# Block-sparse attention with a gated projection behind it: a reserve in the planner's times for work that waits, and another rank for one sequence's value means

## The chip, the cores and the metric

The kernel runs on one core of a Trainium2 chip. The metric is the device time of one execution in microseconds; the number given for a kernel is the median of its runs. A program fixes the order of the instructions on every engine before anything runs. On the chip each engine works through its own list in order and waits where an operand isn't there yet. PE is TensorE, DVE VectorE, ACT ScalarE, POOL GpSimd, and SP is SyncE, whose queue issues the transfers.

## The reference

```python
q, k, v: [4, 8, 768, 64]          # sequences, heads, positions, head width
k_sum = k.reshape(B, H, 24, 32, D).max(axis=3)
v_sum = v.reshape(B, H, 24, 32, D).mean(axis=3)
scores_l = where(|i - j| < 16, scale * q @ k.T, -1e9)
scores_s = scale * q @ k_sum.T + log(32)
a = softmax(concat([scores_l, scores_s], -1))
x = a @ concat([v, v_sum], 2)     # then [B*S, H*D] = [3072, 512]
out = ((x @ w_a) * (x @ w_b)) @ w_out   # w_a, w_b [512, 1536], w_out [1536, 512]
```

Each position sees the positions nearer than 16 and 24 summaries, one for each block of 32 positions: the largest key and the mean value. All is float32. The kernel gets that precision from TensorE with a high and a low part of each factor and three matmuls for each product.

## The kernel before

**Units and tiles.** The 3072 tokens are cut into nine units. The first sequence has three units of two tiles of 128 tokens; the other three sequences have two units of three tiles each. For each unit there is an attention part (scores, softmax, transposes, products with the values) and a projection part of twelve items, one for each 128 columns of `d_ff`. An item has two up projections (line 1046), the elementwise product and its split (`h L1081` and `gl L1086` on VectorE, `g L1078` and `gh` on ScalarE for units of two tiles) and the down projection into the output banks (line 1123). The attention part of a tile is computed beside the items of an earlier unit. Its scores are `c L637`, its products `o L790`.

**The summaries of the values.** `prep_values(b)` computes the value means of sequence b, for four heads at a time. Loads bring values (`S<-in_v`), GpSimd adds them (line 561) and scales the sum (line 588). Four small transfers for the four heads (`S<-vm`) then put the means into the room `summed(b)`, so there are eight for a sequence. `bring` loads the values of a tile into the window `vw` (`vw<-in_v`), and for the first tile of a sequence two transfers (`vw<-S`) put the means into the rows of the window behind the values. The products of that tile read them.

**Queries and transposes.** For each tile, `blocks` loads the queries in 16 small pieces (`qin<-in_q`) and VectorE transposes them (`qT`, line 998). The scores of the tile read `qT`. VectorE scales and masks the scores into `s` (line 666), which frees their banks.

**What sets the order.** The class `Work` gathers operations with an engine, a rank, an estimated duration (`takes`), a delay until others can use the result (`then`) and, for transfers, a rate. `emit` plans the program with these estimates. An operation gets a time `est` at which its operands are there by the plan. For the engine that is free first, `emit` takes the operation of best rank (lowest number) among those whose `est` is not over 0.15 us away:

```python
            op = min(
                (o for o in choices(engine) if o.est <= now + 0.15),
                key=lambda o: (o.rank, o.est, o.index),
            )
```

A table `ORDER` names the first operations of each engine by number; behind these the planner decides. Rank 0 (`CHAIN`) is the chain of copies and multiplications inside an item. On SyncE value loads have rank 97, queries 98 and the `S<-vm` transfers rank 99, the two `vw<-S` rank 97.

Of the kernel before, what the change touches and what calls it, by code (L numbers as in the profile page):

```python
# [16 lines left out]
AX = mybir.AxisListType  # L17
LOG32 = 3.4657359027997265
NEG = -1.0e9

# [39 lines left out]
class Work:  # L62
# [27 lines left out]
    def emit(self):  # L90
        fixed = {e: list(reversed(x)) for e, x in ORDER.items()}
        listed = {i for x in ORDER.values() for i in x}
        ready = {}
        wire = 0.0

        def choices(e):
            ops = ready.get(e, [])
            if fixed.get(e):
                return [o for o in ops if o.index == fixed[e][-1]]
            return [o for o in ops if o.index not in listed]  # L100

        for op in self.ops:
            if not op.left:
                ready.setdefault(op.engine, []).append(op)
        left = len(self.ops)
        while left:
            now, engine = min(
                (max(self.free.get(e, 0.0), min(o.est for o in choices(e))), e)
                for e in ready if choices(e)
# [5 lines that stand above are left out]
            ready[engine].remove(op)  # L115
            left -= 1
            if fixed.get(engine):
                fixed[engine].pop()
            start = max(now, op.est)
            end = self.free[engine] = start + op.takes  # L120
            if op.rate:
                wire = max(wire, end + 1.0) + op.then / op.rate
                end = wire + 0.9
            else:
                end += op.then
            op.start = start
            op.fn()
            for o in op.next:
                o.left -= 1
                same = 0.0 if op.engine == "PE" else 0.12  # L130
                o.est = max(o.est, start + op.takes + same if o.engine == op.engine else end)
                if not o.left:
                    ready.setdefault(o.engine, []).append(o)

# [2 lines left out]
def attention_moe(  # L137
# [19 lines left out]
    NS = S // BLK  # L157
# [21 lines left out]
    def sb(shape, name, dtype=F32):  # L179
        return const.tile(shape, dtype, tag=name, name=name)  # L180
# [28 lines left out]
    def mask_kind(i):  # L209
        for e in range(2):  # L210
            es = slice(e * QT, (e + 1) * QT)

            for c0, n, w in ((0, WIN, 0),) if e == 0 else ((0, 32, 0), (32 + NS, 64, 32)):
# [6 lines left out]
                for step, base, per_query in bounds:  # L220
                    nc.gpsimd.affine_select(
                        out=sl, in_=sl, compare_op=ALU.is_ge, fill=NEG, base=base,
                        pattern=[[step, n]], channel_multiplier=per_query,
# [11 lines left out]
    vbuf = [sb([P, H, D], f"vw{e}") for e in range(2)]  # L235
# [26 lines left out]
    late = []  # L262
# [18 lines left out]
    def summed(b):  # L281
        return spaces["S1"][4 * NS : 5 * NS, 3 * CV :].rearrange("p (h d) -> p h d", d=D)
# [32 lines left out]
    def pool(rank, takes, reads, writes, fn):  # L315
        work.add("POOL", rank, takes, 0.13, reads, writes, fn)

    def load(rank, kb, rate, reads, writes, out, in_):
        work.add(
            "SP", rank, 0.45, kb, reads, writes,  # L320
            lambda: nc.sync.dma_start(out=out, in_=in_), rate=rate,  # L321
        )
# [227 lines left out]
    def prep_values(b):  # L550


        T = 8

        at, keys, rank = (0, ["S1.0", "S1.1"], LATER) if b == 1 else (3, ["S1.3"], 50)
        x = spaces["S1"][: 4 * NS, at * CV :]

        def add(n, out, i0, i1, writes):
            pool(
                rank, 0.15 + n / 450, (), writes,  # L560
                lambda: nc.gpsimd.tensor_tensor(out=out, in0=i0, in1=i1, op=ALU.add),  # L561
            )

        room = ["S1.3"] if b == 1 else []
        work.add("-", 0, 0, 0, (), room, lambda: None)
        for hg in range(2):
            vv = v[b, 4 * hg : 4 * hg + 4].rearrange("h (n t) d -> (h n) t d", t=BLK)
            y, pk = vm[: 4 * NS, hg], f"vm{hg}"
            for i in range(BLK // T):
                j = i % len(keys)  # L570
                load(
                    90, 197.0, 150, (), [keys[j]],
                    x[:, j * T * D : (j + 1) * T * D].rearrange("p (t d) -> p t d", d=D),
                    vv[:, i * T : (i + 1) * T, :],
                )
                if j == len(keys) - 1:
                    n = len(keys) * T * D // 2
                    while n > D:
                        add(n, x[:, :n], x[:, :n], x[:, n : 2 * n], keys)
                        n //= 2  # L580
                    if i == j:
                        add(n, y, x[:, :n], x[:, n : 2 * n], keys + [pk])
                    else:
                        add(n, x[:, :n], x[:, :n], x[:, n : 2 * n], keys)
                        add(n, y, y, x[:, :n], keys + [pk])
            pool(
                rank, 0.37, (), [pk],
                lambda y=y: nc.gpsimd.tensor_scalar(
                    out=y, in0=y, scalar1=1.0 / BLK, scalar2=None, op0=ALU.mult
                ),  # L590
            )
            for h in range(4):
                load(
                    99, 6.0, 20, [pk] + room, [VS[4 * hg + h]],
                    summed(b)[:, 4 * hg + h], y[h * NS : (h + 1) * NS],
                )

# [227 lines left out]
    VK = [f"v{i}" for i in range(5)]  # L825
    VS = [f"vs.{h}" for h in range(H)]
# [136 lines left out]
    def attention(u):  # L963

        b, t0, n = chunks[u]
        rank = rank_of(u)
        banks, vbank = ["c0", "c1"], ["c0", "c1"] if u == FILL else ["o3"] * n
        if t0 == 0:
            prep_keys(b)
            prep_values(b)  # L970
        qk = []
        old = [f"qin.{c}.{r}" for c in range(NP) for r in range(0, P, 32)]
        if n == G:
            for c in range(NP):
                qk += blocks(
                    98, f"qin.{c}", qin[:, c, :], q, b, c, t0 * P, ["lo8"] if u == FILL else ()
                )

        def place(i):
            return slice((t0 + i) % 2 * P, ((t0 + i) % 2 + 1) * P)  # L980

        def bring(i):
            load_values(b, t0 + i, vbuf, VK[:3], 97)
            if t0 == 0 and i == 0:
                for e, r0 in ((0, WIN), (1, 32)):
                    load(97, 49.0, 100, VS + (["S1.3"] if b == 1 else []), [VK[3 + e]], vbuf[e][r0 : r0 + NS], summed(b))

        def begin(i):
            keys = list(qk)
            if n != G:  # L990
                for c in range(NP):
                    keys += blocks(
                        98, f"q{(t0 + i) % 2}.{c}", qin[:, c, place(i)], q, b, c, (t0 + i) * P, (),
                        old if chunks[u - 1][2] == G and i < 2 else (),
                    )
            dve(
                rank_of(u, t0 + i) - 0.05 * (u > FILL), 0.62, keys, ["qT"],
                lambda: nc.vector.transpose(out=qTs, in_=qin[:, :, place(i)]),
            )
            scores(u, t0 + i, qTs, "qT", s0, SK, banks, lead=lead.pop() if lead else None)  # L1000

        def turned(i):
            transposes(u, t0 + i, s0, SK, banks)

        def end(i):
            pt = (pown, [PU, ["S0.2", "S0.3"]]) if u == FILL and i else None
            return u, t0 + i, vbuf, VK, vbank[i], pt

        if u == FILL:

            yield
            bring(0)
            begin(0)
            turned(0)
            yield
            begin(1)
            pool(rank, 0.9, (), ["S0.2", "S0.3"], lambda: nc.gpsimd.memset(pown, 0.0))
            turned(1)
            yield
            values(*end(0))  # L1020
            bring(1)
            values(*end(1))
        else:
            for i in range(n):
                begin(i)
                bring(i)
                turned(i)
                if u == FILL + 1:
                    values(*end(i))
                else:  # L1030
                    lead.append(products(*end(i)))
        if u == NU - 1:
            reads, bk, fn, split = lead.pop()
            pe(-1, 1.1, reads, [bk], fn)
            split()
        yield
# [203 lines left out]
```

## Time and profile before

| what | value |
| --- | --- |
| median of three runs | 673.56 us (675.9, 673.56, 672.68) |
| the profiled execution | 675.08 us, its span 673.3 us, mean granted clock of TensorE 0.983 |
| PE busy | 646.2 us, 96% of the span |
| PE weight loads busy | 603.3 us, 90% (beside the matmuls) |
| DVE busy | 401.9 us, 60% |
| ACT busy | 244.5 us, 36% |
| POOL busy | 156.4 us, 23% |

The span is cut into 40 slices on the page, and each digit tells a slice's busy share, or for the clock its granted share of full speed, in tenths (9 is 90% or more). A timeline row gives the start and the duration in microseconds, then the line, the operation, the tiles written and read, and how many instructions are taken together; in brackets stands how long the engine was idle before them and what ended that. A row of the chain of waits gives one piece of the work that ended last. SPq is the time in which SyncE issues a transfer, not the transfer itself.

### The profile page before, as it was taken

The numbers are of one execution on the slowest core, as the hardware profiler recorded it, in microseconds if no ns is written. First come the engines' busy times: TensorE is split into PE (matmuls) and PEld (weight loads), VectorE is DVE, ScalarE is ACT, GpSimd is POOL, SyncE is SP. The second block draws the span as 40 slices with busy tenths as digits, with TensorE's granted clock in tenths as the row PEclk, the third lists the DMA queues.
The fourth block names the chain that finished last, engine by engine and source line by source line (L and its number), as shares of the span: only waits on it lengthen the run. The fifth ranks groups of instructions, "written<-read, shape, count | busy, mean of one in ns | idle before, by whom it ended". The sixth has DMA issues, their size and how long they took to land.

```text
span 673.3 us, 13320 instructions
## 1 busy us (share of the span) xinstructions
PE 646.2 (96%) x5096; PEld 603.3 (90%) x5096; DVE 401.9 (60%) x880; ACT 244.5 (36%) x725; POOL 156.4 (23%) x236
## 2 busy tenths in 40 slices
PE   6699999999699999999999999999999999999997
PEld 5589898998689999999999999999999999999996
DVE  5787799967177777477776865776762542222212
ACT  4798685333134331233333413333331411121111
POOL 5767466351033444211111100101110100000000
PEclk9689999999989999999999999999999999999999
DMA  9997995532134235332222431222000200010001
GB/s 206 255 301 182 359 259 95 114 93 63 27 85 105 62 67 98 75 91 42 40 40 41 94 61 36 39 63 55 11 21 1 70 1 1 0 48 1 1 0 48
DMA packets 154664, 54.73 MB, mean 81 GB/s; under 512 B 134745, under 2 KB 147289, under 8 KB 154601
## 3 DMA queue, kind: packets, MB, share of 16 engines
q1 hardware_dynamic: 154456, 53.75, 33.4%
q8 instruction: 40, 0.66, 0.4%
q14 instruction: 24, 0.19, 0.1%
q10 hardware_dynamic: 144, 0.13, 0.1%
HBM read 47.12 MB, written 6.29 MB: 79 GB/s over the span
## 4 chain that ended last, share of the span: by engine, by line
PE 77%; SPq 7%; DMA 6%; DVE 5%; issue 2%; ACT 1%; POOL 1%; POOLq 0%; ACTq 0%; DVEq 0%
PE h L1046 46%; PE o L1123 24%; SPq L321 7%; PE o L790 3%; DMA raw<-in_moe_w_a_dram 3%; PE c L637 2%; DMA raw<-in_moe_w_out_dram 2%; DVE S L774 1%; POOL w L403 1%; DVE pt L774 1%; DVE c L387 1%; DVE S L395 1%; DVE h L1081 1%; PE o L624 0%; PE o L637 0%
## 5 line engine op out<-in xcount | busy, mean ns | idle before, releaser
L1046 PE MATMUL h<-x,w 128*128 128x384 f32 (+1 forms) x2292 | 392.0, 307 | 0.0
L1046 PEld LDWEIGHTS h<-x,w 128*128 128x128 f32 x2292 | 342.9, 190 | 4.7 <-issue 0.3
L1123 PE MATMUL o<-w,gh 128*128 128x512 f32 x498 | 123.8, 383 | 0.1
L1109 DVE TENSOR_TENSOR h<-h,g 128x384 f32<-128x384 f32 x71 | 40.2, 566 | 134.8 <-PE h L1046 134.4
L1111 ACT CAST gh<-h 128x384 fp32r<-128x384 f32 x71 | 34.0, 479 | 214.2 <-DVE h L1109 209.1
L774 DVE STREAM_TRANSPOSE pt<-s 32x256 f32<-32x256 f32 x228 | 99.3, 436 | 20.7 <-POOL s L729 10.0
L1123 PEld LDWEIGHTS o<-w,gh 128*128 128x128 f32 x498 | 90.6, 189 | 11.5 <-issue 1.9
L729 POOL TENSOR_TENSOR s<-s,nml 128x480 f32<-128x480 f32 x44 | 43.3, 988 | 236.2 <-DVE nml L725 187.6
L1046 PE MATMUL h<-late,w 128*128 128x384 f32 x288 | 93.9, 326 | 0.0
L703 ACT ACTIVATE s<-s,nml 128x120 f32<-128x120 f32 x160 | 61.3, 386 | 33.7 <-DVE nml L674 33.7
L1123 PE MATMUL o<-w,gl 128*128 128x512 f32 x249 | 68.7, 381 | 0.0
L1046 PEld LDWEIGHTS h<-late,w 128*128 128x128 f32 x288 | 54.4, 189 | 0.9
L1106 ACT COPY g<-h 128x384 f32<-128x384 f32 x72 | 34.5, 480 | 55.1 <-PE h L1046 54.3
L1123 PEld LDWEIGHTS o<-w,gl 128*128 128x128 f32 x249 | 46.6, 189 | 7.4 <-DVE gl L1086 0.6
L1114 DVE TENSOR_TENSOR gl<-h,gh 128x384 fp32r<-128x384 f32 x71 | 39.4, 555 | 22.1 <-ACT gh L1111 21.3
L561 POOL TENSOR_TENSOR S<-S 96x256 f32<-96x256 f32 (+3 forms) x58 | 33.2, 572 | 67.6 <-DMA S<-in_v_dram 64.6
L666 DVE SCALAR_TENSOR_TENSOR s<-c,mask 128x480 f32<-128x480 f32 x40 | 26.1, 652 | 20.5 <-PE c L637 20.3
L403 POOL TENSOR_TENSOR w<-S,w 128x512 fp32r<-128x512 f32 x24 | 30.7, 1285 | 9.9 <-ACT w L400 8.8
L1123 PE MATMUL o<-w,x 128*128 128x512 f32 x117 | 30.9, 400 | 0.6 <-POOL w L403 0.5
L703 ACT ACTIVATION_READ_ACCUMULATOR s<-s,nml 128x1 f32 x160 | 30.3, 189 | 0.0
L1078 ACT COPY g<-h 128x256 f32<-128x256 f32 x36 | 13.4, 373 | 46.1 <-PE h L1046 46.1
L387 DVE TENSOR_SCALAR c<-raw 128x512 int32<-128x512 uint32 x36 | 27.3, 761 | 1.6 <-DMA raw<-in_moe_w_a_dram 1.0
(130 smaller groups left out, 527.0 us busy)
## 6 DMA issues: line engine op xcount, KB each, us to landing
raw<-in_moe_w_b_dram SPq DMA_DIRECT2D x12, 512.0 KB
raw<-in_moe_w_a_dram SPq DMA_DIRECT2D x12, 512.0 KB
raw<-in_moe_w_out_dram SPq DMA_DIRECT2D x12, 512.0 KB
out_dram<-S SPq DMA_DIRECT2D x23, 256.0 KB
qin<-in_q_dram SPq DMA_DIRECT2D x288, 16.0 KB
S<-in_v_dram SPq DMA_DIRECT2D x24, 192.0 KB
kin<-in_k_dram SPq DMA_DIRECT2D x38, 100.0 KB
vw<-in_v_dram SPq DMA_DIRECT2D x17, 192.0 KB
```

Of the source, the lines that this page charges most:

```text
L321: lambda: nc.sync.dma_start(out=out, in_=in_), rate=rate,
L387: dve(rank, 0.66, [raw], [bk], lambda: nc.vector.tensor_scalar(out=z.bitcast(I32), in0=word(0).bitcast(U32), scalar1=2.0**-29, scalar2=7.0 ...
L403: lambda eng=nc.vector if near else nc.gpsimd: eng.tensor_tensor(out=half(1), in0=t, in1=half(0).bitcast(F32), op=ALU.subtract),
L703: lambda h=h, c=c, more=more: nc.scalar.activation(y[h][:, c, :], x[h][:, c, :], AF.Exp, bias=m[:, 0, h, c : c + 1], scale=1.0, **more,),
L729: lambda h=h, r=r: nc.gpsimd.tensor_tensor(out=y[h], in0=y[h], in1=r[:, :, None].broadcast_to([P, NP, COLS]), op=ALU.mult,),
L774: lambda js=js, qs=qs, rs=rs: nc.vector.transpose(out=pv[js, rs, qs], in_=sv[qs, rs, js]),
L1046: nc.tensor.matmul(ps, w[:, c, part, :], inputs_of(u, xpart)[:, :, c].rearrange("p g (a b) -> p g b a", a=2), start=(i == 0), stop=(i == n ...
L1106: act(CHAIN, 0.13 + W / 1030, ["h0"], gk, lambda: nc.scalar.copy(out=g, in_=pa))
L1109: lambda: nc.vector.tensor_tensor(out=pb, in0=pb, in1=g, op=ALU.mult),
L1111: act(CHAIN, 0.16 + W / 1030, [bk], [ghk], lambda: nc.scalar.copy(out=gh, in_=pb))
L1114: lambda: nc.vector.tensor_tensor(out=gl, in0=pb, in1=gh.bitcast(F32), op=ALU.subtract),
L1123: nc.tensor.matmul(bank[ok[j]], (gh if first else gl)[:, j * P : (j + 1) * P], w[:, :, part, :].rearrange("p (z a) n -> p z n a", a=2), st ...
```

## The change

The planner gets a constant `SLACK`. When an operation ends and another one waits for it on another engine, the time at which the second one can start by the plan is set later: by 0.35 us if the first is work of an engine, and by 2.0 us if it is a transfer. This holds only for times beyond 70 us of the plan, and neither for operations of rank 0 nor for those of SyncE. Apart from that, for sequence 1 (the second one) the eight `S<-vm` get rank 89 in place of 99 and the two `vw<-S` rank 89.5 in place of 97, so that both stand before the queries with 98. In the changed kernel all lines behind the planner are four higher.

```diff
--- before.py
+++ after.py
@@ -17,6 +17,7 @@
 AX = mybir.AxisListType
 LOG32 = 3.4657359027997265
 NEG = -1.0e9
+SLACK = (0.35, 2.0)
 
 
 
@@ -128,7 +129,10 @@
             for o in op.next:
                 o.left -= 1
                 same = 0.0 if op.engine == "PE" else 0.12
-                o.est = max(o.est, start + op.takes + same if o.engine == op.engine else end)
+                late = start + op.takes + same if o.engine == op.engine else end
+                if late > 70 and o.rank and o.engine != "SP" and o.engine != op.engine:
+                    late += SLACK[op.rate > 0]
+                o.est = max(o.est, late)
                 if not o.left:
                     ready.setdefault(o.engine, []).append(o)
 
@@ -591,7 +595,7 @@
             )
             for h in range(4):
                 load(
-                    99, 6.0, 20, [pk] + room, [VS[4 * hg + h]],
+                    89 if b == 1 else 99, 6.0, 20, [pk] + room, [VS[4 * hg + h]],
                     summed(b)[:, 4 * hg + h], y[h * NS : (h + 1) * NS],
                 )
 
@@ -983,7 +987,7 @@
             load_values(b, t0 + i, vbuf, VK[:3], 97)
             if t0 == 0 and i == 0:
                 for e, r0 in ((0, WIN), (1, 32)):
-                    load(97, 49.0, 100, VS + (["S1.3"] if b == 1 else []), [VK[3 + e]], vbuf[e][r0 : r0 + NS], summed(b))
+                    load(89.5 if b == 1 else 97, 49.0, 100, VS + (["S1.3"] if b == 1 else []), [VK[3 + e]], vbuf[e][r0 : r0 + NS], summed(b))
 
         def begin(i):
             keys = list(qk)
```

Every engine executes the same instructions as before, in another order. The explicit order comes first in both, and the first differences stand behind it.

SyncE's queue around the second sequence's means, before (`S_146<-vm` are the means, `S_146<-in_v_dram` the values that they are computed from, `qin` the queries, `out_dram` the second unit's output in the row that follows the 30 queries):

```order
L321 DMA S_146<-vm 24x64 x3
L321 DMA S_146<-in_v_dram 96x512 x2
L321 DMA S_146<-vm 24x64
L321 DMA qin<-in_q_dram 32x4x32 x30
L321 DMA out_dram<-S_147 128x512 x2
L321 DMA qin<-in_q_dram 32x4x32 x34
L321 DMA S_146<-vm 24x64 x4
L321 DMA vw_129<-S_146 24x512
L321 DMA vw_130<-S_146 24x512
```

The same place now:

```order
L325 DMA S_146<-vm 24x64 x4
L325 DMA vw_130<-in_v_dram 64x8x64
L325 DMA qin<-in_q_dram 32x4x32 x2
L325 DMA S_146<-in_v_dram 96x512 x2
L325 DMA out_dram<-S_147 128x512 x2
L325 DMA qin<-in_q_dram 32x4x32 x11
L325 DMA S_146<-vm 24x64 x4
L325 DMA vw_129<-S_146 24x512
L325 DMA vw_130<-S_146 24x512
```

Between the second four `S<-vm` and the loads of their values there are 11 queries now, where there were 64. The two queries of the shown row with x2 belong to the second sequence's second tile; they stood ahead of the first four `S<-vm` and now come behind them.

TensorE's queue at the products of the second sequence's first tile (`o_74<-pt,vw_129`, the first two rows of eight), before:

```order
L1123 MATMUL o_71<-w_870,gh 128x512 x2
L1123 MATMUL o_72<-w_870,gh 128x512 x2
L1123 MATMUL o_71<-w_870,gl 128x512
L1123 MATMUL o_72<-w_870,gl 128x512
L1046 MATMUL h_75<-x,w_1064 128x256 x12
L1046 MATMUL h_75<-x,w_1020 128x256 x12
L790 MATMUL o_74<-pt,vw_129 64x64 x2
L790 MATMUL o_74<-pt,vw_130 64x64 x2
```

The same products now:

```order
L1050 MATMUL h_76<-x,w_693 128x256 x12
L1050 MATMUL h_76<-x,w_706 128x256 x12
L1127 MATMUL o_71<-w_699,gh 128x512 x2
L1127 MATMUL o_72<-w_699,gh 128x512 x2
L1127 MATMUL o_71<-w_699,gl 128x512
L1127 MATMUL o_72<-w_699,gl 128x512
L794 MATMUL o_74<-pt,vw_129 64x64 x2
L794 MATMUL o_74<-pt,vw_130 64x64 x2
```

They stood behind the up projection with `w_1064` and now follow the down projection with `w_699`, which is four items' places further up. The scores of the third tile, which stood ahead of that down projection, come behind the products.

TensorE's queue at the scores of the second sequence's second tile (the last two rows of eight, `c_77` and `c_78`) and what follows them, before (`o_73` and `o_74` are the second unit's last down projection):

```order
L637 MATMUL c_77<-kT,qT 64x120 x2
L637 MATMUL c_78<-kT,qT 64x120 x2
L1046 MATMUL h_75<-x,w_450 128x256 x12
L1046 MATMUL h_75<-x,w_399 128x256 x12
L1123 MATMUL o_73<-w_1393,x 128x512 x2
L1123 MATMUL o_74<-w_1393,x 128x512 x2
L1123 MATMUL o_73<-w_1393,x 128x512
L1123 MATMUL o_74<-w_1393,x 128x512
```

The same place now:

```order
L1127 MATMUL o_73<-w_1393,x 128x512 x2
L1127 MATMUL o_74<-w_1393,x 128x512 x2
L1127 MATMUL o_73<-w_1393,x 128x512
L1127 MATMUL o_74<-w_1393,x 128x512
L1050 MATMUL h_75<-x,w_450 128x256 x12
L1050 MATMUL h_75<-x,w_399 128x256 x12
L641 MATMUL c_77<-kT,qT 64x120 x2
L641 MATMUL c_78<-kT,qT 64x120 x2
```

The last down projection of the second unit and the up projection with `w_450` (shown whole) have gone ahead of all eight rows of these scores.

## Rows read from the trace of the kernel before

**Rows 1.** The page: busy time of TensorE, and its granted clock in 40 slices.

```profile
PE 646.2 (96%) x5096; PEld 603.3 (90%) x5096; DVE 401.9 (60%) x880; ACT 244.5 (36%) x725; POOL 156.4 (23%) x236
...
PEclk9689999999989999999999999999999999999999
```

**Rows 2.** Stretches of the span: length, busy of PE, PEld, DVE, ACT, POOL, clock, DMA.

```profile
170.00:187.00 17.00, 11.45 (x103) 10.78 (x103) 2.62 (x7) 2.61 (x7) 0.03 (x1) 0.89 0.18 36
187.00:204.00 17.00, 17.00 (x168) 15.30 (x165) 13.05 (x29) 5.63 (x22) 6.99 (x13) 0.91 0.31 75
400.00:663.00 263.00, 263.00 (x1821) 249.80 (x1820) 108.52 (x232) 66.17 (x193) 12.47 (x14) 1.00 0.10 24
```

**Rows 3.** Waits of TensorE: us in total, times, longest.

```profile
PE o L790 <- DMA vw<-S: 5.6, 2, 5.4
```

**Rows 4.** Timeline of SyncE, 100 to 190 us.

```profile
138.96 2.50 SPq L321 DMA_DIRECT2D S<-vm  x3
141.55 0.92 SPq L321 DMA_DIRECT2D S<-in_v_dram  x2
...
143.38 15.74 SPq L321 DMA_DIRECT2D qin<-in_q_dram  x30
...
160.12 18.36 SPq L321 DMA_DIRECT2D qin<-in_q_dram  x34
178.58 3.05 SPq L321 DMA_DIRECT2D S<-vm  x4
182.90 1.48 SPq L321 DMA_DIRECT2D vw<-S  x2
```

**Rows 5.** The chain that ended last, 66 to 190 us: start, us, what.

```profile
151.17 0.43 SPq L321
151.65 1.72 DMA qin<-in_q_dram
...
183.67 2.07 DMA vw<-S
```

**Rows 6.** Stretches of 2 us, columns as in the other stretches.

```profile
162.00:164.00 2.00, 0.71 (x9) 0.29 (x12) 1.97 (x4) 0.62 (x3) 0.00 (x0) 1.00 0.25 43
...
184.00:186.00 2.00, 0.70 (x8) 0.54 (x10) 0.00 (x0) 0.00 (x0) 0.00 (x0) 0.50 0.36 98
```

**Rows 7.** Timeline of TensorE, 100 to 200 us.

```profile
106.13 1.05 PE L637 MATMUL c<-kT,qT 64*64 64x120 f32 x32 [1.53 <-DVE qT L998]
...
148.85 1.05 PE L637 MATMUL c<-kT,qT 64*64 64x120 f32 x32
...
152.61 1.46 PE L1123 MATMUL o<-w,x 128*128 128x512 f32 x6
...
162.66 0.42 PE L637 MATMUL c<-kT,qT 64*64 64x120 f32 x4 [0.46 <-DVE s L666]
163.91 1.04 PE L637 MATMUL c<-kT,qT 64*64 64x120 f32 x28 [0.83 <-DVE s L666]
...
166.28 5.52 PE L1046 MATMUL h<-x,w 128*128 128x256 f32 x48
...
185.11 0.48 PE L790 MATMUL o<-pt,vw 120*64 120x64 f32 x4 [5.37 <-DMA vw<-S]
185.78 1.76 PE L790 MATMUL o<-pt,vw 120*64 120x64 f32 x28 [0.19 <-DMA vw<-S]
187.47 2.76 PE L1123 MATMUL o<-w,x 128*128 128x512 f32 x6
...
196.82 1.15 PE L790 MATMUL o<-pt,vw 120*64 120x64 f32 x32
```

**Rows 8.** Timeline of GpSimd, 136 to 190 us.

```profile
145.01 3.02 POOL L561 TENSOR_TENSOR S<-S 96x512 f32<-96x512 f32 x4 [5.05 <-DMA S<-in_v_dram]
...
148.51 0.37 POOL L588 TENSOR_SCALAR vm<-vm 96x64 f32<-96x64 f32 x1
```

**Rows 9.** Timeline of VectorE, 148 to 165 us.

```profile
153.45 0.71 DVE L998 STREAM_TRANSPOSE qT<-qin 128x512 f32<-128x512 f32 x1 [2.74 <-DMA qin<-in_q_dram]
```

## The prediction

> **What bounds the kernel now.** I read the busy shares of the page first. TensorE is at work for 646.2 us of a 673.3 us span, and its granted clock is high in all but a few slices [rows 1]. A change that leaves the number of matmuls alone can therefore win only time in which TensorE stands idle or runs at its lower clock. Next I cut the span into stretches of 17 us, to see where that time lies. From 187 us to 663 us TensorE is busy in every microsecond. The stretch of 170 to 187 has 11.45 us of 17 [rows 2]. The ramp before 66 us is held by the explicit order, which the change leaves as it is. The third view is the list of TensorE's waits: the longest behind the ramp is for the transfer `vw<-S`, the second sequence's value means on their way into the value window [rows 3].
>
> The queue of SyncE says why they are late. The first half of the means was issued around 139 us and its sums' second half was loaded at 141.55. Then come 30 query blocks, two outputs and 34 more query blocks, and only at 178.58 the second four `S<-vm` [rows 4]. GpSimd had those means ready at 148.51 + 0.37 = 148.9 us [rows 8]. So they sat for 30 us behind work of better rank. `vw<-S` reads what they write, so it is issued at 182.90, and lands 2.07 us after its second issue [rows 4, 5]. TensorE waits 5.37 + 0.19 us, and runs at half clock afterwards [rows 6, 7].
>
> **What the change does and what each part costs.** Every engine gets the instructions that it had. Only their order differs, and only behind the explicit order.
>
> *The means.* The eight `S<-vm` now rank ahead of queries. By the new order the second four have 182 transfers ahead of them on SyncE, not 219, and none is skipped or doubled. Of those 182, 180 are the ones that stood first before too, and two are the second unit's outputs. The 180 were out at about 157.7: the 34 queries begin at 160.12 after 185 transfers, and the three queries and two outputs before that take some 2.4, at 0.475 us from one query to the next [rows 4, 5]. With the two outputs the means can be issued at 158.7. They need their sums. The two loads that feed these have 17 more transfers ahead than before, in places that came at 151.2, so they end at 152.1 [rows 5]. GpSimd started 2.5 us after such a pair and took 3.87 us [rows 4, 8], which gives 158.5, just in time. The outputs need their copies, and by the new order the second unit's last down projection stands ahead of an up projection of 2.8 us and a score group, so the copies come earlier as well. From the first `S<-vm` to the products took 185.78 - 178.58 = 7.2 us [rows 4, 7], so the window is whole at **165.9**.
>
> TensorE would meet the products there at **167**: in the new order they follow the down projection with `w_699`, ahead of which the up projection with `w_693` now stands. That began at 166.28, right behind the other, and is half of 5.52 [rows 7]; so 166.28 + 2.7, less the third tile's scores that have gone behind the products (1.05) and their waits (1.29), less 1.0 and plus 1.5 for the two scores below. That is a margin of about 1 us. The wait of **5.56 us goes**; the bounds are 0 and 2 us of it left.
>
> *The clock.* The six down matmuls behind the products took 2.76 us where six others took 1.46, and 28 product matmuls 1.76 where 32 take some 1.1, so 28 some 0.95 [rows 7]. That is 1.30 + 0.81 = **2.1 us** at half clock, after a stretch in which TensorE did nothing [rows 6, 7]. Waits of 0.46, 0.83 and 1.53 us left the clock whole (1.00 in 162 to 164, with 1.29 us idle) [rows 6, 7]. So if the new waits are of that size, the 2.1 us go too. The Trainium skill (TensorE: Matmul & The Clock Gate, "A second HAM failure mode: psum-queue depth-cycling") says that frequent short idles between groups of matmuls can throttle the clock as well; by that, the short waits left here could cost what the long one did, and the sum would be 2.1 us smaller. The row of 162 to 164 speaks against it.
>
> *Scores of the third tile.* They waited 0.46 + 0.83 us for VectorE to read the banks [rows 7]. With the reserve the planner sets them behind the products, some 7 us later, while VectorE's order is nearly the same. **1.29 us go**; bounds 0.5 and 1.3.
>
> *First scores of the third unit.* They waited 1.53 us for their transposed queries [rows 7]. By the new order four matmuls of a down projection stand ahead, two thirds of a group of 1.46. **1.0 us go**; bounds 0 and 1.53.
>
> *What comes new.* Three queries of the second tile move from issue 139 to 141 (about 133 us) to 157, 165 and 166, behind the four first means. Issue 166 was out by 151.1, landing took 1.7 us and the transpose takes 0.7 [rows 5, 9]: the scores can start at 153.5. TensorE got to them at 148.85; the down projection (to 154.1) and the up projection now go first, so it comes at 154.1 - 1.05 - 1.0 = 152.0 [rows 7]. **A new wait of 1.5 us**; bounds 0 and 3, since VectorE waited 2.74 us in the same way for the next tile's queries, unseen by TensorE [rows 9].
>
> *The reserve behind 187 us.* It reorders work there too, but TensorE has no idle time to win. A new order costs something only if TensorE meets an operand that isn't there. The reserve plans work for other engines later, never earlier, and the projections' own copies are excluded, so I cost it at nothing. The cover is TensorE's backlog of down and up projections; without it each late operand costs its lateness.
>
> **The sum.** 5.56 + 2.1 + 1.29 + 1.0 - 1.5 = 8.45, so 8.5 us. The profiled execution took 675.08 us, so it becomes 666.6. The median of the three runs is 1.52 us below that execution, so I predict **665.1 us**.
>
> **The rivals.**
> *The wait only shrinks.* The margin of 1 us is thin on both sides. SyncE loses about 1 us now and then: its 30 queries took 15.74 us where 30 x 0.475 is 14.25 [rows 4]. The sums come only 0.2 us before their transfer. If the means are late by 4 us, TensorE idles for 3 there, since it now arrives some 17 us sooner. It gains 5.5 us in all: 669.6 at the profiled execution's level less 1.5, so 668. If the wait is again as long as 5.4, the clock falls again too: 665.1 + 5.4 + 2.1 = 672.6, no gain to speak of. I give 0.11 to 667 to 670, and 0.06 to the second.
> *Short waits throttle.* By the rows of 162 to 164 it doesn't happen; if it did, 2.1 us stay: 667.2. Chance 0.04.
> *The change does not reach the bound.* The planner goes by its own times, so on the chip the same means could wait elsewhere; but the order itself shows them 37 places further up. 673.6, chance 0.03.
> *Slower.* SyncE issues in order. The first four `S<-vm` now stand ahead of two of the second tile's queries. If GpSimd's sums are late, SyncE stands at the first `S<-vm`, and all queries with it; VectorE then stands at the transpose of those queries, and the multiplications (`h L1081`) that feed TensorE are queued behind it. It has happened here in small: VectorE idled 2.74 us for queries [rows 9]. The price is 1 us for each microsecond beyond the 1.5 already counted, plus 2.1 for the clock. It makes the kernel slower by over 0.5% from 9.8 us on (8.5 + 3.4 - 2.1), so if the queries land behind 162.6 in place of 152.8; 12 us would give 679. For it: GpSimd waited 5.05 us for a load in this stretch [rows 8]. Against it: the first means could be issued at 138.96 before [rows 4], and now go at about 146. Chance 0.05.
>
> **How the numbers follow.** My forecast has 0.71; its own range, from the bounds of the terms, is 663 to 668. A measurement of this kernel can tell about 0.5%, 3.4 us. Faster means under 670.2: 0.71 + 0.11 + 0.04 - 0.03 for the upper end = 0.83. Same is 0.06 + 0.03 + 0.03 = 0.12, slower 0.05. Leaving out the cases above, the range is **662.8 to 670**.
>
> **What would show it.** In the changed profile the wait of `o L790` for `vw<-S` should be gone or under 2 us, the clock 1.00 from 170 to 204, `S<-vm` issued near 159, a wait of 1 to 2 us at the scores near 152 for `qT`, and no wait for `s L666` at 162. Behind 200 us TensorE stays full. A wait of over 3 us for `vw<-S` near 167 makes the first rival right; idle time behind 200 us makes my cost of the reserve wrong, and idle VectorE with TensorE behind it near 150 the last one.

## The result

The changed kernel takes **663.47 us** (median of four runs, 663.15 to 664.12), the kernel before 673.12 us on the same chip: a ratio of 0.9853, with a 95% interval of 0.982 to 0.9885. Measured again beside the experiments it took 663.08 us (0.9846, 0.9821 to 0.9872). The forecast was 665.1 us, in a range of 662.8 to 670.

| the profiled execution | before | changed |
| --- | --- | --- |
| its time / its span | 675.08 / 673.3 us | 664.12 / 662.3 us |
| PE busy | 646.2 us, 96% | 642.8 us, 97% |
| mean granted clock | 0.983 | 0.992 |

The page of the changed kernel, TensorE's busy time and clock; they answer to [rows 1]:

```profile
PE 642.8 (97%) x5096; PEld 600.8 (91%) x5096; DVE 401.8 (61%) x880; ACT 243.6 (37%) x725; POOL 156.3 (24%) x236
...
PEclk9789999999999999999999999999999999999999
```

TensorE's waits behind the ramp, in the changed kernel (total, times, longest). What was 5.6 us for `vw<-S` in [rows 3] is 0.5:

```profile
PE c L641 <- DVE qT L1002: 0.7, 1, 0.7
PE c L641 <- DVE nml L723: 0.6, 1, 0.6
PE o L794 <- DMA vw<-S: 0.5, 1, 0.5
```

The stretches that answer to [rows 2]. From 170 to 187 us TensorE now works in every microsecond, at full clock:

```profile
153.00:170.00 17.00, 16.45 (x144) 15.00 (x143) 11.96 (x28) 5.72 (x22) 7.33 (x12) 1.00 0.21 40
170.00:187.00 17.00, 17.00 (x198) 15.73 (x197) 13.65 (x33) 6.75 (x27) 5.66 (x11) 1.00 0.35 73
187.00:204.00 17.00, 17.00 (x154) 16.09 (x154) 11.69 (x29) 6.42 (x25) 6.65 (x11) 1.00 0.39 83
400.00:652.00 252.00, 252.00 (x1759) 239.29 (x1758) 107.86 (x231) 64.02 (x189) 12.58 (x15) 1.00 0.11 26
```

SyncE's timeline in the changed kernel, for [rows 4]. Eleven queries stand between the loads of the values at 148.55 and the second four `S<-vm`, which are issued at 156.38 and no longer at 178.58:

```profile
148.55 0.83 SPq L325 DMA_DIRECT2D S<-in_v_dram  x2
...
150.85 5.40 SPq L325 DMA_DIRECT2D qin<-in_q_dram  x11
156.38 3.09 SPq L325 DMA_DIRECT2D S<-vm  x4
```

GpSimd's timeline there, for [rows 8]: the scaled sums end at 155.99 + 0.37 = 156.36, and SyncE issues the means at once.

```profile
152.48 3.02 POOL L565 TENSOR_TENSOR S<-S 96x512 f32<-96x512 f32 x4 [12.17 <-DMA S<-in_v_dram]
...
155.99 0.37 POOL L592 TENSOR_SCALAR vm<-vm 96x64 f32<-96x64 f32 x1
```

TensorE's timeline, for [rows 7]. The scores of the second tile stand at 150.88, the products at 163.99 and 164.85, the scores of the third tile, which had waited twice, at 170.27 without a wait. The six down matmuls behind the products took 2.76 us before and take 1.85 now, and the next start 1.69 us behind them. The granted clock is 1.00 there; the last two of the six start at 166.97, right behind VectorE's `x L1090`, which ends at 166.91:

```profile
104.80 1.05 PE L641 MATMUL c<-kT,qT 64*64 64x120 f32 x32 [0.67 <-DVE qT L1002]
...
150.88 1.05 PE L641 MATMUL c<-kT,qT 64*64 64x120 f32 x32 [0.60 <-DVE nml L723]
...
163.99 0.34 PE L794 MATMUL o<-pt,vw 120*64 120x64 f32 x4
164.85 1.04 PE L794 MATMUL o<-pt,vw 120*64 120x64 f32 x28 [0.53 <-DMA vw<-S]
165.81 1.85 PE L1127 MATMUL o<-w,x 128*128 128x512 f32 x6
...
170.27 1.05 PE L641 MATMUL c<-kT,qT 64*64 64x120 f32 x32
```

The row at 150.88 names `nml L723` as what ended the wait, an operation of 0.13 us that stands right behind the transpose of that tile's queries. VectorE had waited 1.78 us for these queries, and their transpose ended at 150.11 + 0.71 = 150.82:

```profile
150.11 0.71 DVE L1002 STREAM_TRANSPOSE qT<-qin 128x512 f32<-128x512 f32 x1 [1.78 <-DMA qin<-in_q_dram]
```

The two profiled executions are 10.96 us apart. Idle time of TensorE from 102 us on went from 8.56 to 1.87 us, which is 6.69, and the half clock was 2.1. Another 1.0 us was there at 75 us, where nothing has moved yet: a down projection that waits for GpSimd's weights began at 75.11 before, at 74.11 now, at 73.70 when the changed kernel was profiled again and at 75.43 in a run with the order of the kernel before up to that place. So the ramp varies by over 1 us from one execution to the next, and the medians, 9.65 us apart, are the better measure of the change. Some 0.35 us more came by 97 us; 0.8 us I could not assign.

### The profile page after: what moved, and what is told of

The parts are those of the page before. It is cut to its first block, busy times and chain, and to the rows that moved or that the text cites. A ratio compares the mean times of both kernels' runs of the same rounds, so it can differ in the third digit from the quotient of the medians.

```text
span 662.3 us, 13323 instructions
## 1 busy us (share of the span) xinstructions
PE 642.8 (97%) x5096; PEld 600.8 (91%) x5096; DVE 401.8 (61%) x880; ACT 243.6 (37%) x725; POOL 156.3 (24%) x236
## 4 chain that ended last, share of the span: by engine, by line
PE 81%; DVE 6%; DMA 5%; SPq 4%; ACT 1%; issue 1%; POOL 1%; DVEq 0%; ACTq 0%; POOLq 0%
PE h L1050 49%; PE o L1127 25%; SPq L325 4%; PE o L794 3%; PE c L641 3%; DMA space<-in_q_dram 2%; DVE S L399 2%; DVE c L391 2%; DMA raw<-in_moe_w_a_dram 1%; DMA raw<-in_moe_w_b_dram 1%; DVE h L1085 1%; DMA S<-in_v_dram 1%; DVE S L778 0%; DMA S<-vm 0%; PE o L628 0%
## 5 line engine op out<-in xcount | busy, mean ns | idle before, releaser
L733 POOL TENSOR_TENSOR s<-s,nml 128x480 f32<-128x480 f32 x44 | 43.4, 988 | 219.8 <-DVE nml L729 196.0
```

What stands on the lines that cost most here:

```text
L733: lambda h=h, r=r: nc.gpsimd.tensor_tensor(out=y[h], in0=y[h], in1=r[:, :, None].broadcast_to([P, NP, COLS]), op=ALU.mult,),
```

## The experiments

Two questions were open. Which part of the change brings the gain, the ranks or the reserve? And what does the reserve do, if TensorE has no idle time behind 187 us? In all of them the lines are those of the changed kernel, unless told. The planner makes a whole new order for each edit of its constants, so each run shows one order, and what differs from run to run is not one operation alone.

**The ranks alone.**

```diff
-SLACK = (0.35, 2.0)
+SLACK = (0.0, 0.0)
```

> The two new ranks alone, the reserve set to 0 and 0. Theory A (the ranks bring the gain, the reserve only moves small waits): the second four S<-vm have 172 transfers ahead, an issue that came at about 153.3 us before, and 7.2 to 8.5 us later the window is whole: 160.5 to 162. TensorE meets the products where it met the third tile's scores before less a down projection, at about 160.6, so 0 to 1.4 us of the wait are left, the clock stays whole, and the time is 665.5 to 667.5 us. Theory B (without the reserve the plan sets work right behind the moment at which its operands are there by the plan, so the wait for vw<-S is replaced by others, for ScalarE's gh, VectorE's copies or the scores' banks): over 4 us of idle time behind 150 us, 669 us or more.

Measured: 679.15 us, a ratio of 1.0083 (1.0051 to 1.0116) to the kernel before: **slower** than before, far on the side of theory B. The wait for `vw<-S` is gone; others stand in its place. All engines around the largest:

```profile
167.17 1.65 POOL L565 TENSOR_TENSOR S<-S 96x256 f32<-96x256 f32 x3 [4.86 <-DMA S<-in_v_dram]
...
169.18 0.98 POOL L733 TENSOR_TENSOR s<-s,nml 128x480 f32<-128x480 f32 x1
...
170.54 0.99 POOL L733 TENSOR_TENSOR s<-s,nml 128x480 f32<-128x480 f32 x1 [0.38 <-DVE nml L729]
171.56 1.78 DVE L778 STREAM_TRANSPOSE pt<-s 32x256 f32<-32x256 f32 x4 [1.16 <-POOL s L733]
...
173.37 0.43 DVE L1085 TENSOR_TENSOR h<-h,g 128x256 f32<-128x256 f32 x1
...
174.26 2.07 PE L1127 MATMUL o<-w,x 128*128 128x512 f32 x4 [2.83 <-ACT x L1087]
```

GpSimd idles 4.86 us for a load of values, then does its sums, and only then scales the softmax (`s L733`), though VectorE had the factors at 165.6. VectorE stands at the first transpose `pt` (of the scaled softmax, for the products) that needs this, and behind it in VectorE's order stands `h L1085`, the product that the next down projection is made from, by way of ScalarE's copy `x L1087`. TensorE waits 2.83 us. It then runs at the lower level:

```profile
172.00:174.00 2.00, 0.00 (x0) 0.00 (x0) 1.90 (x5) 0.16 (x1) 0.00 (x0) 0.89 0.46 124
...
176.00:178.00 2.00, 2.00 (x8) 1.72 (x8) 1.90 (x6) 0.37 (x1) 0.38 (x2) 0.50 0.20 33
```

At 204 to 221 us the same pattern costs 3.11 us of idle time more. The idle time from 102 us on is 8.52 us, what it was before, and more of the rest is at half clock.

**The reserve alone**, at the old ranks.

```diff
-                    89 if b == 1 else 99, 6.0, 20, [pk] + room, [VS[4 * hg + h]],
+                    99, 6.0, 20, [pk] + room, [VS[4 * hg + h]],
-                    load(89.5 if b == 1 else 97, 49.0, 100, VS + (["S1.3"] if b == 1 else []), [VK[3 + e]], vbuf[e][r0 : r0 + NS], summed(b))
+                    load(97, 49.0, 100, VS + (["S1.3"] if b == 1 else []), [VK[3 + e]], vbuf[e][r0 : r0 + NS], summed(b))
```

> The reserve alone, the means at their old ranks 99 and 97. The second four S<-vm have 203 transfers ahead, 21 more than in the changed kernel, where they went at 156.38: so about 166.5, and with 8.5 us the window is whole at 175. TensorE meets the products, by the matmuls ahead of them, at about 173. Theory A (the ranks bring the gain): the long wait stays, 4 us or more with the clock at half behind it, 669 to 673 us. Theory B (the reserve brings most, since it moves the third tile's scores and other work ahead of the products): a wait of 1 to 3 us, clock whole, 664.5 to 667 us.

Measured: 667.25 us, 0.9908 (0.9882 to 0.9934), just above theory B's range. The wait for `vw<-S` is 0.34 us. The means still follow queries, but 32 of them and no longer 64: without the ranks too SyncE issues the second four `S<-vm` sooner, at 166.84 and not at 178.58. But TensorE idles 2.25 us between 255 and 400 us:

```profile
255.00:400.00 145.00, 142.75 (x1112) 134.14 (x1111) 92.75 (x213) 45.39 (x151) 23.59 (x41) 1.00 0.27 58
```

**The reserve alone, up to 190 us of the plan.**

```diff
-                if late > 70 and o.rank and o.engine != "SP" and o.engine != op.engine:
+                if 70 < late < 190 and o.rank and o.engine != "SP" and o.engine != op.engine:
```

with the ranks as in the run before.

> The reserve alone at the old ranks, and only for times from 70 to 190 us of the plan. With the reserve at all times (667.25 us) TensorE idled 2.25 us between 255 and 400 us, for x L817 and gh L1115, and 0.28 before. Theory A (that loss is made by the reserve's new order behind 190): it is gone, 664 to 666 us. Theory B (it comes with the later means and would be there anyway): 666.5 us or more.

Measured: 664.38 us, 0.9857 (0.9834 to 0.988): all of the change's gain, within what can be told, **without the ranks**. The idle time behind 255 us is gone, so the reserve's own order had made it:

```profile
255.00:400.00 145.00, 145.00 (x1127) 136.63 (x1126) 96.75 (x227) 46.13 (x152) 21.33 (x35) 1.00 0.30 61
```

The products come 10 us later than in the changed kernel and wait 0.18 + 0.34 us. The third tile's scores stand ahead of them, with a wait of 0.93 us like that of before:

```profile
167.31 1.04 PE L641 MATMUL c<-kT,qT 64*64 64x120 f32 x28 [0.93 <-DVE s L670]
...
174.00 0.34 PE L794 MATMUL o<-pt,vw 120*64 120x64 f32 x4 [0.18 <-DMA vw<-S]
174.68 1.04 PE L794 MATMUL o<-pt,vw 120*64 120x64 f32 x28 [0.34 <-DMA vw<-S]
```

Set against the kernel before, both sides of that wait came sooner. TensorE is at the products at 173.8, where it was there at 179.7 [rows 7], and SyncE issues the means 11.1 us sooner, though their ranks are the old ones:

```profile
150.63 16.77 SPq L325 DMA_DIRECT2D qin<-in_q_dram  x32
167.50 3.06 SPq L325 DMA_DIRECT2D S<-vm  x4
```

So the reserve alone moves the transfers as well. Why its plan puts fewer queries ahead of them, no run shows.

**Both, the reserve up to 190 us of the plan** (the condition of the run before, with the new ranks).

> The changed kernel, with the reserve only for times from 70 to 190 us of the plan, so that the work behind is planned without it. Theory A (my prediction: behind 187 us the reserve costs nothing and brings nothing, TensorE is full there either way): within 1 us of the changed kernel, 662.5 to 664.5 us, no wait of TensorE over 0.5 us behind 190. Theory B (the reserve also keeps TensorE full behind 190 us, where the ranks alone lost 3.11 us and half clock at 204 to 221): idle time of 1 to 3 us behind 190, 665 to 669 us.

Measured: 665.12 us, 0.9875 (0.9847 to 0.9904); its interval overlaps that of the changed kernel. In its profile TensorE is busy in every microsecond from 170 us to 655 us. By its time it lies 0.6 above A's range and just inside B's. By its profile A stands: the idle time that B asks for behind 190 us isn't there, while 66 to 102 us has 1.51 us of it, where the changed kernel had 0.66 with the same order.

**The means moved, nothing else.** The order of the kernel before was written out whole in the table `ORDER`, with six transfers moved on SyncE; the lines of this kernel are 122 higher than those of the kernel before. SyncE's queue in short (the table itself holds numbers):

```diff
 qin<-in_q x27
+S<-vm x4, vw<-S x2
 qin<-in_q x3, out_dram<-S x2, qin<-in_q x34
-S<-vm x4, vw<-S x2
```

> The order of the kernel before, written out whole for every engine, with one difference: on SyncE the second four S<-vm and the two vw<-S stand 39 transfers further up, ahead of the transfer that had 180 ahead of it. Nothing else moves on any engine. Theory A (my terms of the sum: the wait and the half clock behind it are paid at this place alone): 5.56 us and 2.1 us go, the other waits stay, 665 to 667 us. Theory B (the stall hid lateness of the other engines behind it: VectorE, ScalarE and GpSimd caught up in the 5.6 us): with the stall gone TensorE idles 2 us or more between 187 and 300 us where it had none, 668 to 673 us.

Measured: 669.6 us, 0.9939 (0.9922 to 0.9955), so 4 us of the 7.7. The stall at the products is gone. The rest is paid at the next tile's products, though not for the engines that theory B had named. SyncE's timeline:

```profile
157.70 3.05 SPq L443 DMA_DIRECT2D S<-vm  x4
...
166.87 17.37 SPq L443 DMA_DIRECT2D qin<-in_q_dram  x34
...
184.81 0.95 SPq L443 DMA_DIRECT2D vw<-in_v_dram  x2
188.47 0.32 SPq L443 DMA_DIRECT2D S<-in_v_dram  x1
188.85 0.69 SPq L443 DMA_DIRECT2D vw<-in_v_dram  x1
```

Behind the 34 queries stand the value loads of the next tile, `vw<-in_v`. Two of the three are issued at 184.81. The third stands behind a load for the value sums, for which SyncE waits until GpSimd has freed the buffer at 188.46, and so goes at 188.85. The kernel before issued that third load no sooner, but came to these products only at 196.82 [rows 7]. Its row on SyncE:

```profile
189.01 0.69 SPq L321 DMA_DIRECT2D vw<-in_v_dram  x1
```

With the means moved TensorE is there sooner and idles 2.72 us ahead of them (`L912` is `L790` here):

```profile
191.85 1.13 PE L912 MATMUL o<-pt,vw 120*64 120x64 f32 x28 [2.72 <-DMA vw<-in_v_dram]
```

From 193 to 195 us the granted clock is 0.50. So the stall of 5.56 us had hidden another late transfer of the same queue.

**The two halves of the reserve**, with the ranks: `SLACK = (0.35, 0.0)`, then `SLACK = (0.0, 2.0)`.

> The ranks, and the reserve of 0.35 us for results of engines alone (none for transfers). Theory A: the reserve's parts matter little, within 1.5 us of the changed kernel (662 to 665 us). Theory B (the reserve for transfers is what keeps work off operands that land later than planned): the second four S<-vm now have 159 transfers ahead, only 15 behind the loads of their values, and TensorE meets the products 1.3 us sooner than in the changed kernel; so a wait of 2 to 4 us at vw<-S and 666 to 669 us.

Measured: 670.67 us, 0.9961 (0.9945 to 0.9978), above theory B's range, and not by its wait. All engines around the longest:

```profile
162.64 0.71 DVE L1002 STREAM_TRANSPOSE qT<-qin 128x512 f32<-128x512 f32 x1 [8.27 <-DMA qin<-in_q_dram]
...
165.97 0.34 PE L794 MATMUL o<-pt,vw 120*64 120x64 f32 x4 [4.27 <-DVE pt L778]
...
167.76 0.43 DVE L1085 TENSOR_TENSOR h<-h,g 128x256 f32<-128x256 f32 x1
...
169.17 1.12 PE L794 MATMUL o<-pt,vw 120*64 120x64 f32 x16 [2.87 <-DVE pt L778]
```

Without a reserve for transfers VectorE reaches the transpose of queries (`qT`) 8.27 us before they land, and the `pt` that TensorE's products need, and `h L1085`, are queued behind it. This is the mechanism of my slower rival.

> The ranks, and the reserve of 2.0 us for transfers alone (none for engines). Theory A: within 1.5 us of the changed kernel (662 to 665 us). Theory B (both halves of the reserve count): the second four S<-vm have 177 transfers ahead and go at about 155.5, the window is whole at 163 to 164, TensorE is there at about 160, so 3 us of wait and beyond it some idle time for gh or the scores' banks; 666.5 to 669 us.

Measured: 665.49 us, 0.9881 (0.9856 to 0.9907), between the theories and 2.0 to 2.4 us above the changed kernel's two medians. Of the 15.7 us that the whole reserve takes off the ranks alone (679.15 to 663.47) the 2.0 us for transfers bring 13.7 by themselves, the 0.35 us for engines 8.5; the two overlap.

**The reserve by the engine that gets it**, with the ranks. The condition `o.engine != "SP"` becomes, in turn, `o.engine not in ("SP", "POOL")`, `o.engine == "POOL"`, `o.engine == "DVE"` and `o.engine not in ("SP", "DVE")`.

> The changed kernel, but work of GpSimd is planned without a reserve. Theory G (the reserve earns by keeping GpSimd's value sums, which wait for loads, from standing ahead of its softmax scaling, for which VectorE's transposes and TensorE wait in turn, as in the run with the ranks alone): GpSimd waits 3 us or more for S<-in_v ahead of s L733, TensorE idles 2.5 us or more for it, 667 to 674 us. Theory V (the reserve earns on VectorE, by keeping the query transposes behind work that feeds TensorE): within 2 us of the changed kernel, 662 to 665.5 us.

> The changed kernel, but only work of GpSimd is planned with the reserve. Theory G: most of the gain stays, 662.5 to 667 us. Theory V: VectorE stands 3 us or more at a query transpose (qT) or at pt with the multiplications behind it, TensorE idles 4 us or more, 668 us or more.

> The changed kernel, but only work of VectorE is planned with the reserve. Theory G: GpSimd's sums stand in the way as with the ranks alone, TensorE idles 4 us or more, 670 to 680 us. Theory V: most of the gain stays, 662.5 to 667 us.

> The changed kernel, but work of VectorE is planned without a reserve; GpSimd's and TensorE's keep it. Theory G (the reserve earns on GpSimd): within 2 us of the changed kernel, 662 to 666 us, with no wait of GpSimd for S<-in_v that TensorE feels. Theory V (it earns on VectorE): VectorE stands at qT or pt ahead of the multiplications that feed TensorE, 667 us or more.

| the reserve holds for | us | ratio to before |
| --- | --- | --- |
| all but SyncE (the change) | 663.47, again 663.08 | 0.9853, 0.9846 |
| all but SyncE and VectorE | 664.55 | 0.9864 (0.9841 to 0.9886) |
| GpSimd alone | 667.55 | 0.9912 (0.9889 to 0.9936) |
| all but SyncE and GpSimd | 670.49 | 0.9949 (0.9931 to 0.9967) |
| VectorE alone | 671.81 | 0.9982 (0.9967 to 0.9997) |
| none (ranks alone) | 679.15 | 1.0083 (1.0051 to 1.0116) |

Theory G holds in its direction: with GpSimd's work planned without a reserve, two thirds of the gain over the kernel before are lost, and without VectorE's some 1 us. GpSimd alone does not carry all of it (667.55, where G allowed up to 667), and VectorE alone takes 7.3 us off the ranks alone, so the engines' shares overlap as well. The run with all but GpSimd fell within G's time, with the same chain, though its longest wait is 1.91 us where G asked for 2.5. All engines' timeline of that run:

```profile
204.18 0.72 POOL L565 TENSOR_TENSOR S<-S 96x256 f32<-96x256 f32 x1 [3.50 <-DMA S<-in_v_dram]
...
207.01 0.98 POOL L733 TENSOR_TENSOR s<-s,nml 128x480 f32<-128x480 f32 x1
...
208.03 0.43 DVE L778 STREAM_TRANSPOSE pt<-s 32x256 f32<-32x256 f32 x1 [5.69 <-POOL s L733]
...
209.25 2.39 PE L1127 MATMUL o<-w,x 128*128 128x512 f32 x5 [1.91 <-ACT x L1087]
```

With VectorE alone too: a value load holds GpSimd for 6.87 us, VectorE, which had already stood 4.32 us at a query transpose, waits 3.78 us for `s L733`, and TensorE 3.58 us for VectorE.

```profile
167.81 0.71 DVE L1002 STREAM_TRANSPOSE qT<-qin 128x512 f32<-128x512 f32 x1 [4.32 <-DMA qin<-in_q_dram]
...
169.05 1.65 POOL L565 TENSOR_TENSOR S<-S 96x256 f32<-96x256 f32 x3 [6.87 <-DMA S<-in_v_dram]
...
172.90 0.88 DVE L778 STREAM_TRANSPOSE pt<-s 32x256 f32<-32x256 f32 x2 [3.78 <-POOL s L733]
...
174.29 1.20 PE L1127 MATMUL o<-w,x 128*128 128x512 f32 x2 [3.58 <-DVE x L1090]
```

**The changed kernel again.**

> The changed kernel as it is, beside the others on the same chip, for what its ramp and its times vary by: 662.5 to 664.5 us. In its profiled execution the ramp up to 102 us may differ from the first one by some 1 us, since no order differs there before 82 us.

Measured: 663.08 us, as above. No run beat it; the reserve alone up to 190 us comes within 1.3 us of it.

## Why the prediction was right, and where its reason failed

The time was right, since the sum was made on the order of the whole change. Its terms, one by one:

*The wait for `vw<-S`.* Forecast to go, bounds 0 and 2: 0.53 us are left. The means could be issued at 156.38, where I had 158.7, and the window was whole at 164.85, where I had 165.9; from the first `S<-vm` it took 8.5 us and not 7.2, as the landing of the means took 3.06 us. But TensorE came at 164.3, not at 167, so the margin of 1 us was a wait of half a microsecond. Both sides came sooner than forecast, which is in part luck: of TensorE's 2.7 us, 1.35 were there by 97 us and 0.9 are the new wait below. Still sooner means would have won next to nothing: VectorE's transpose `pt` for these products ended at 162.50 + 2.24 = 164.74, the transfer at 164.76, and in the second profile of the changed kernel the 0.47 us of waiting there ended with `pt`.

*The clock.* The 2.1 us went; the clock is 1.00 in every stretch from 102 us on.

*The scores.* The third tile's lost both waits (1.29 us). The third unit's still wait 0.67 us, where I left 0.53 (0.38 in the second profile).

*The new wait* for the second tile's queries was 0.60 us, not 1.5, the largest miss among the terms: 0.9 us. In the second profile TensorE does not wait there. The 0.53 us at the products and 0.14 at the third unit's scores take most of that back, so the terms explain 0.2 of the 1.6 us by which the forecast was too high. Another 0.44 is the median of the kernel before, 673.56 over three runs and 673.12 over four. The rest is no more than the ramp varies by.

*The reserve behind 187 us at nothing* held for the change. It is not a rule: alone, at the old ranks, the reserve cost 2.25 us of idle time there.

**The step that failed is the cause.** Under "The means" the rank was to bring the 5.56 us, and the clock with it, and the reserve stood in the sum only for two small waits of scores. The runs show the reverse. The ranks alone make the kernel slower by 0.8%; the reserve alone, up to 190 us of the plan, makes it as fast as the change. The transfer's place in SyncE's queue was a right reading of the wait: wherever the means came sooner it went or was under 0.6 us, and with the ranks alone it went whole. Two things were wrong. The rank was not needed to bring them sooner, since the plan with the reserve does so by itself (167.50 against 178.58). And bringing them sooner does not earn the wait and its half clock by itself, because other waits follow. The experiment that moved the means by themselves shows one of these: behind the stall stood another late transfer of the same queue. What the ranks add to the reserve depends on how far it reaches: 3.8 us if it holds at all times (667.25 to 663.47), and nothing that can be told if it ends at 190 us (664.38 against 665.12).

The reserve works against a pattern that the list of TensorE's waits hides. GpSimd takes sums whose load hasn't landed, VectorE stands at a transpose for GpSimd, and the product that TensorE needs is queued behind that transpose. It comes with the order that the planner makes when the ranks alone change, and not with the earlier means as such: with the means moved by themselves, TensorE waited at most 0.5 us for a `gh` or its copy.

*The rivals.* That short waits throttle did not happen in the changed kernel. It did elsewhere, below, so my argument from the row of 162 to 164 us was too strong. The slower rival's mechanism, VectorE at the head of its queue with TensorE's work behind, did not happen in the change beyond the 0.60 us, and did in four of the other runs: at a query transpose with the reserve for engines only and with VectorE alone, at `pt` with the ranks alone, with VectorE alone and with all but GpSimd.

## What to carry to other kernels

When a plan of static times moves one operation forward, look at each in-order queue for what will be at its head when that operation is done: a wait that goes can uncover the next one. A reserve on results that cross engines, above all on transfers and for the engine that others wait for, is worth trying alone, before ranks are tuned by hand. And an edit with two parts should be run in its parts even when the sum comes out right.

## What the hardware showed that I had not expected

The granted clock does not follow the length of the single wait (each case here is one profiled execution). In the kernel before, a wait of 1.53 us at the third unit's scores left it at 1.00. With the reserve for GpSimd alone, 1.71 us at the same place was followed by the lower level (1.2 GHz), and six down matmuls took 2.50 us in place of 1.46:

```profile
104.65 1.05 PE L641 MATMUL c<-kT,qT 64*64 64x120 f32 x32 [1.71 <-DVE qT L1002]
105.63 2.50 PE L1127 MATMUL o<-w,x 128*128 128x512 f32 x6
```

```profile
106.00:110.00 4.00, 4.00 (x12) 3.22 (x11) 3.93 (x16) 2.68 (x14) 2.11 (x3) 0.57 0.38 96
```

With the reserve for transfers alone 1.49 and 0.41 us of waiting before the products were followed by 0.50 at 162 to 164 us. But with the reserve for VectorE alone 2.47 us of waiting, up to 212.60, left it at 1.00:

```profile
211.00:213.00 2.00, 0.40 (x2) 0.38 (x3) 1.91 (x5) 0.75 (x2) 1.68 (x5) 1.00 0.00 0
213.00:215.00 2.00, 1.53 (x10) 0.80 (x8) 1.90 (x6) 0.59 (x1) 0.09 (x1) 1.00 0.29 101
```

The Trainium skill (TensorE: Matmul & The Clock Gate, "A second HAM failure mode: psum-queue depth-cycling") tells of a kernel whose TensorE idles briefly between groups of matmuls, often enough that its clock goes down and up. The changed kernel's three short waits, 0.67, 0.60 and 0.53 us and far apart, left the clock at 1.00; the 0.57 from 106 to 110 us stands behind a single wait, so no run here shows that pattern.

A forecast of the clock behind a wait of 1.5 to 2.5 us should keep both outcomes. By the stretch above they are 1.7 us apart (0.43 of 4 us; an estimate).
